# Linear-attention block with a SwiGLU feed-forward: a denser kv sum, whole-tile attention in four PSUM banks, layer-norm small ops on POOL

## Chip, cores and metric

One core of a Trainium2 chip. The metric is device time in microseconds of the whole kernel; 248.45 us is the median of three runs of the kernel before (248.22 to 249.34).

## The reference

One sequence of 2048 tokens, width 512, 32 heads of 16, feed-forward width 1376, all in bf16. `c` gives six modulation vectors.

```python
mod = (silu(c) @ w_mod)                       # -> sa, ca, ga, sb, cb, gb
h = layernorm(x) * (1 + ca) + sa
q, k, v = split(h @ wqkv)                     # 32 heads of 16
pq, pk = q @ w_phi, k @ w_phi                 # per head 16 x 16
phi = concat(softmax(p), softmax(-p))         # per head 32 features
kv, z = sum_s(phi_k * v), sum_s(phi_k)        # per head 32 x 16, 32
o = (phi_q @ kv) / (phi_q . z + 1e-6)
x = x + ga * (o @ wo)
h = layernorm(x) * (1 + cb) + sb
x = x + gb * ((silu(h @ w_gate) * (h @ w_up)) @ w_down)
```

## The kernel before

Tokens go in 16 tiles of 128 (a tile's tokens lie across the partitions), in four chunks of 512. The work falls into a first pass over all tiles, which ends in the kv sum, and a second one with attention, projection and feed-forward.

**First pass.** `first_norm` takes the mean and variance of each tile on VectorE (`stats`: two instructions), adds epsilon on VectorE, takes the power -0.5 on POOL and computes -mean*rstd on VectorE (`rstd_of`), for groups of two, two, four, four and four tiles; `normalize` runs on VectorE or ScalarE. TensorE transposes the tile, and the evacuation applies the modulation (`modulate_T`). `k_tile` multiplies by the key weights (with w_phi folded in by `fold_phi`) and the value weights; ScalarE takes exp of both signs into `e`; VectorE sums per head (`S`) and takes reciprocals (`R`); POOL multiplies (`phik`, L551). `kv_tile` adds phik^T [v, 1] into PSUM over all tiles: eight matmuls a tile, each with the 128 features of eight heads of one sign against 128 value columns and a column of ones. Three banks hold the sums: the pair `two_ps` and one single bank. `q_front` makes exp(+-q) per chunk and column block. `gate` broadcasts ga and gb, and POOL scales wo (four pieces, L626) and w_down (eleven, L630) by them as soon as they are there.

**KVZ** (`fz`, L642 and L645): VectorE multiplies the sums by a block mask and writes the matrix that the attention multiplies by: per sign and block of eight heads 128 columns of kv, eight columns of head masks and eight of z plus epsilon.

**Second pass.** `attend(n, half)` works on half a tile in the pair of banks: four matmuls, two small copies (`Ssw`), then U, den, rden, A on small operands and two multiplies `o` (L707) that read PSUM, all on VectorE (the copies on ScalarE from the third tile on). The pair is free for the next half when `o` is done. `turn` transposes the result, `project` multiplies by wo, adds to x and does the second layer norm; `second_T` transposes and modulates. `ffn_gu` does gate and up (two single banks), ScalarE silu and then either VectorE's multiply or a ScalarE copy and POOL's multiply; `ffn_down` sums eleven matmuls, and VectorE adds x. `UNITS` lists the feed-forward's units as (chunk, first tile, tiles).

**Order.** All work is given to a planner (`Plan`) as operations with engine, an estimated duration, buffers read and written. It computes due times backwards over successors (`STRETCH`, `WAIT`), the TensorE spine (`SPINE`) and the paced preparations (`PACE`, us between pairs of tiles), then places operations one by one on the engines in a simulated time and emits the instructions in that order; each engine then runs its own queue in order. `slots` says how many buffers a kind has, and `quota` how many single PSUM banks a purpose may hold. PSUM has eight banks: the pair and six single ones.

## Time and profile before

| | |
|---|---|
| profiled execution | 248.46 us |
| its span, first to last instruction | 246.7 us |
| TensorE, VectorE, ScalarE, POOL busy | 215.0, 174.6, 128.3, 101.1 us |
| mean granted TensorE clock | 0.979 |

The span was cut into four stages at 9.3 us (the modulation weights have landed), 58.4 and 72.1 us (the last kv matmul) and 92.2 us (the first gate/up matmul). A line of the stage view reads: start:end, length, busy us and instructions of TensorE's matmuls, its weight loads, VectorE, ScalarE and POOL, then the granted clock (1.00 is 2.4 GHz, with 1.2 GHz as the other level), the share of the DMA engines and GB/s. PE is TensorE, DVE VectorE, ACT ScalarE; L548 is line 548 of the kernel. A group's row gives the shapes, the count, busy time, the mean duration of one in ns, and the idle time before them with what ended it.

### The profile page before, as it was taken

Reading aid. Unit: us, or ns where it says so; the run is one execution under the profiler, and the core shown is the slowest. Engines: PE = TensorE matmul, PEld = TensorE weight load, DVE = VectorE, ACT = ScalarE, POOL = GpSimd, SP = SyncE. Lnnn points to the kernel's source line nnn. Section 1 sums busy time; section 2 is a strip of 40 time slices with the busy share of each in tenths; the row PEclk is TensorE's granted clock in tenths of the full one; section 3 lists DMA queues with packets and bytes.
Section 4 is the critical chain, followed back from the end, with each engine's and each line's share of the span. In section 5 each row is a group of like instructions: output and inputs, shape, how many; then the busy total and the mean of one; then the engine's idle time right before and its main releaser. Section 6 shows DMA issues by size and latency. Waiting matters only on the chain.

```text
span 246.7 us, 4221 instructions
## 1 busy us (share of the span) xinstructions
PE 215.0 (87%) x1533; PEld 131.7 (53%) x1556; DVE 174.6 (71%) x461; ACT 128.3 (52%) x280; POOL 101.1 (41%) x100
## 2 busy tenths in 40 slices
...
DMA packets 9062, 13.95 MB, mean 57 GB/s; under 512 B 1009, under 2 KB 6482, under 8 KB 9042
## 3 DMA queue, kind: packets, MB, share of 16 engines
...
q8 instruction: 12, 0.20, 0.3%
...
## 4 chain that ended last, share of the span: by engine, by line
PE 64%; DVE 24%; ACT 3%; DMA 3%; issue 3%; POOL 1%; SPq 0%; DVEq 0%; ACTq 0%
PE one_ps L786 31%; PE one_ps L818 14%; DVE S L548 5%; PE one_ps L748 5%; PE two_ps L675 3%; DVE st L343 3%; DMA wmod_sb<-in_w_mod_dram 3%; DVE xn L372 3%; PE one_ps L528 2%; PE one_ps L575 2%; DVE R L549 2%; PE one_ps L532 2%; DVE o L707 2%; ACT hT L396 2%; DVE ln_nmr L361 1%
## 5 line engine op out<-in xcount | busy, mean ns | idle before, releaser
L786 PE MATMUL one_ps<-hT,wg_sb 128*128 128x256 bf16 (+3 forms) x264 | 46.2, 308 | 1.2 <-ACT hT L396 0.9
L786 PE MATMUL one_ps<-hT,wu_sb 128*128 128x256 bf16 (+3 forms) x260 | 45.2, 307 | 0.2
L793 ACT ACTIVATE sg<-one_ps 128x512 bf16<-128x512 f32 (+2 forms) x46 | 26.3, 577 | 28.3 <-PE one_ps L786 25.2
L802 POOL TENSOR_TENSOR gu<-usb,sg 128x512 bf16<-128x512 bf16 (+1 forms) x22 | 23.5, 1070 | 42.7 <-ACT usb L800 39.9
L818 PE MATMUL one_ps<-wd_sb,gu 128*128 128x512 bf16 (+1 forms) x171 | 40.5, 379 | 0.2
L551 POOL TENSOR_TENSOR phik<-e,R 128x1024 bf16<-128x1024 bf16 x16 | 30.7, 1931 | 13.0 <-ACT hT L396 5.5
L786 PEld LDWEIGHTS <-wg_sb 128*128 128x128 bf16 (+1 forms) x264 | 25.9, 100 | 13.9 <-issue 2.1
L786 PEld LDWEIGHTS <-wu_sb 128*128 128x128 bf16 (+1 forms) x264 | 26.0, 100 | 12.2
L736 POOL TENSOR_TENSOR o<-o 128x512 bf16<-128x512 bf16 x14 | 16.1, 1152 | 38.0 <-DVE o L707 33.6
L796 DVE TENSOR_TENSOR gu<-one_ps,sg 128x512 bf16<-128x512 f32 (+1 forms) x24 | 16.3, 685 | 20.3 <-PE one_ps L786 18.4
L357 POOL TENSOR_TENSOR ln_rstd<-ln_veps,mhalf 128x1 f32<-128x1 f32 (+2 forms) x21 | 13.4, 639 | 38.3 <-DVE ln_veps L353 33.7
L818 PEld LDWEIGHTS <-gu 128*128 128x128 bf16 (+1 forms) x176 | 16.7, 98 | 17.0
L707 DVE TENSOR_TENSOR o<-two_ps,A 128x256 bf16<-128x256 f32 x64 | 24.0, 416 | 0.8
L343 DVE BATCH_NORM_STATS2 st<-x_c 128x6 f32<-128x512 bf16 x32 | 21.7, 679 | 2.7 <-DMA x_c<-in_A_x_dram 2.4
L581 ACT ACTIVATE eT<-one_ps 128x512 bf16<-128x512 f32 x32 | 17.5, 599 | 10.3 <-PE one_ps L575 10.3
L675 PE MATMUL two_ps<-KVZ,eT 128*128 128x144 bf16 x128 | 13.7, 232 | 7.3 <-DVE o L707 6.9
L548 DVE TENSOR_REDUCE S<-e 128x64 f32<-128x1024 bf16 x16 | 19.1, 1191 | 1.3 <-ACT e L539 1.2
L388 PE MATMUL one_ps<-ident_b,xn 128*128 128x128 bf16 x128 | 11.9, 236 | 7.1 <-DVE va L544 3.9
L528 PE MATMUL one_ps<-Wk,hT 128*128 128x512 bf16 x61 | 17.2, 399 | 1.0 <-ACT hT L396 0.6
L532 PE MATMUL one_ps<-wqkv_sb,hT 128*128 128x512 bf16 x62 | 17.1, 391 | 0.3 <-DVE st L343 0.2
L675 PEld LDWEIGHTS <-eT 128*128 128x128 bf16 x128 | 10.0, 100 | 13.6 <-DVE o L707 6.0
L748 PE MATMUL one_ps<-wo_sb,oT 128*128 128x512 bf16 x58 | 15.6, 380 | 1.7 <-ACT oT L739 1.4
...
## 6 DMA issues: line engine op xcount, KB each, us to landing
...
```

Source lines behind the costliest of these rows:

```text
L343: nc.vector.bn_stats(st6[:], src)
L528: nc.tensor.matmul(pk()[:], lhsT=hT[c_i][k][:, cols], rhs=Wk2[:, k, :], start=(k == 0), stop=(k == KD - 1))
L532: nc.tensor.matmul(v()[:], lhsT=hT[c_i][k][:, cols], rhs=wqkv_sb[:, k, 2 * D:3 * D], start=(k == 0), stop=(k == KD - 1))
L548: pl.op("DVE", r=[e], w=[Ss], us=1.18, fn=lambda: nc.vector.tensor_reduce(Ss()[:], e()[:], axis=AX.X, op=ALU.add))
L551: pl.op("POOL", r=[e, R], w=[bphik[i]], us=1.9, fn=lambda: nc.gpsimd.tensor_tensor(bphik[i]()[:], e()[:], R()[:].unsqueeze(3).to_broadcast ...
L675: nc.tensor.matmul(nd()[:, jj, sg * NDW:(sg + 1) * NDW], lhsT=eTs[c_i, sg, j][:, ts_], rhs=KVZ[:, sg * KD + j, :], start=True, stop=True)
L707: nc.vector.tensor_tensor(o2()[:, sg, half * HK:(half + 1) * HK, :].rearrange("p j (h d) -> p j h d", d=DH), ndv()[:, :, sg, 0:P].rearrang ...
L748: nc.tensor.matmul(a()[:], lhsT=oT()[:, j, :], rhs=wo_sb[:, j, :], start=(j == 0), stop=(j == KD - 1))
L786: nc.tensor.matmul(ps_()[0:fsz, q * n:(q + 1) * n], lhsT=wt[:, k, m * P:m * P + fsz], rhs=h2[k], start=(k == 0), stop=(k == KD - 1))
L793: pl.op("ACT", r=[g, bsilu], w=[sg], us=0.2 + 0.3 * L / CW, fn=lambda: nc.scalar.activation(sg()[0:fsz, 0:L], g()[0:fsz, 0:L], ACT.Silu))
L802: pl.op("POOL", r=[usb, sg], w=[gu], us=0.1 + 1.05 * L / CW, fn=lambda: nc.gpsimd.tensor_tensor(gu()[0:fsz, 0:L], usb()[0:fsz, 0:L], sg()[ ...
L818: nc.tensor.matmul(fp()[:], lhsT=b()[0:fsz, c0:c0 + P], rhs=wd_sb[0:fsz, m, :], start=(m == 0), stop=(m == FM - 1))
```

## The change

- The kv sum takes the features of four heads, both signs, in one matmul against the 64 value columns of these heads and a column of ones; eight matmuls a tile as before, with 65 columns instead of 129. The sums fit in two banks (`kv_ps`). `e`, `phik` and `va` are laid out for it, and KVZ is written in four steps, which move rows between partition halves.
- `attend(n)` does a whole tile in four banks (`four_ps`), with the same number of VectorE instructions per tile as per half before. These banks exist only after the kv sum: they take the place of `kv_ps` and of two of the six single banks, which the kinds named in `EARLY` use before.
- The first layer norm's aggregation, power and -mean*rstd run as ten small POOL instructions per group; the second one keeps the aggregation on VectorE and does the rest in four POOL instructions.
- The scaling of wo waits for the last phik, that of w_down for the first step of KVZ.
- Quotas, planner constants and estimates are others, an operation with a choice of engine takes the one that ends it first, gate operations are due before those of two groups later (`soft`), and the two two-tile units of chunk 1 become one of four.

```diff
-UNITS = [(0, 0, 2), (0, 2, 2), (1, 0, 2), (1, 2, 2), (2, 0, 4), (3, 0, 4)]
+HG = 4 * DH
+UNITS = [(0, 0, 2), (0, 2, 2), (1, 0, 4), (2, 0, 4), (3, 0, 4)]
...
-STRETCH = 1.6
-WAIT = 0.8
-SPINE = 1.2
-PACE = 11.0
+STRETCH = 2.54
+WAIT = 1.43
+SPINE = 1.1
+PACE = 8.1
+QUOTA = {'q': 2, 'turn': 4, 'T': 2, 'T2': 4, 'wo': 4, 'down': 4, 'gu': 3, 'kv': 4, 'fold': 2}
+EARLY = ("kv", "q", "fold", "T")
...
+            if b.tag == "one" and not (b.kind == f"last{i - 4}" if str(b.kind)[:4] == "last" else i < 4 or b.kind in EARLY):
+                continue
...
-    slots = {"one": 6, "two": 1, "xn": 8, "nmr": 4, "ln2": 6, "WT": 2, "e": 3, "S": 3, "R": 3, "phik": 4,
+    slots = {"one": 6, "four": 1, "xn": 8, "nmr": 4, "ln2": 6, "WT": 2, "e": 3, "S": 3, "SS": 3, "Q": 3, "R": 3, "phik": 4,
...
-    quota = {"q": 1, "turn": 1, "T": 2, "wo": 1, "down": 2, "gu": 4, "kv": 4, "fold": 3}
+    quota = QUOTA
...
-    two_ps = ps.tile([P, 2, CW], FP32, name="two_ps")
-    one_ps = [ps.tile([P, CW], FP32, name=f"one_ps{i}") for i in range(slots["one"])]
+    early_cm = tc.tile_pool(name="early", bufs=1, space=PSUM)
+    early = early_cm.__enter__()
+    kv_ps = early.tile([P, 2, CW], FP32, name="kv_ps")
+    one_ps = [ps.tile([P, CW], FP32, name=f"one_ps{i}")[:] for i in range(4)]
+    one_ps += [early.tile([P, CW], FP32, name=f"one_ps{i}")[:] for i in range(4, 6)]
+    blast = [Buf("one", kind=f"last{i}", keep=True) for i in range(2)]
+    four_ps = {}
...
-        b0, b, bn = Buf(), Buf(), Buf()
+        bn = Buf()
         st = {}
 
-        def f1():
-            st["veps"] = lnp.tile([P, n], FP32, name=name + "_veps", bufs=bufs)
-            nc.vector.tensor_scalar_add(st["veps"][:], mv_t()[:, :, 1], LN_EPS)
-
-        def f2():
+        def f():
             st["rstd"] = lnp.tile([P, n], FP32, name=name + "_rstd", bufs=bufs)
-            nc.gpsimd.tensor_tensor(st["rstd"][:], st["veps"][:], mhalf[:, 0:n], op=ALU.pow)
-
-        def f3():
             st["nmr"] = lnp.tile([P, n], FP32, name=name + "_nmr", bufs=bufs)
-            nc.vector.scalar_tensor_tensor(st["nmr"][:], in0=mv_t()[:, :, 0], scalar=-1.0, in1=st["rstd"][:],
-                                           op0=ALU.mult, op1=ALU.mult)
-        pl.op("DVE", r=bmv, w=[b0], us=0.1, fn=f1)
-        pl.op("POOL", r=[b0], w=[b], us=0.4 + 0.15 * n, fn=f2)
-        pl.op("DVE", r=[b] + list(bmv), w=[bn], us=0.1, fn=f3)
+            veps = lnp.tile([P, n], FP32, name=name + "_veps", bufs=bufs)
+            nc.gpsimd.tensor_scalar_add(veps[:], mv_t()[:, :, 1], LN_EPS)
+            nc.gpsimd.tensor_tensor(st["rstd"][:], veps[:], mhalf[:, 0:n], op=ALU.pow)
+            nc.gpsimd.tensor_scalar(veps[:], mv_t()[:, :, 0], -1.0, None, op0=ALU.mult)
+            nc.gpsimd.tensor_tensor(st["nmr"][:], veps[:], st["rstd"][:], op=ALU.mult)
+        pl.op("POOL", r=bmv, w=[bn], us=0.8 + 0.15 * n, fn=f)
...
-        pl.op([("DVE", 0.6, fd), ("ACT", 0.71, fa)], r=list(reads) + [bn], w=[bxn])
+        pl.op([("DVE", dve_us, fd), ("ACT", 0.72, fa)], r=list(reads) + [bn], w=[bxn])
...
+        st6 = lnp.tile([P, w, 6], FP32, name=f"ln1_st{n0}")
+        bst = [Buf() for _ in range(w)]
         for q in range(w):
             c_i, t = divmod(n0 + q, TPC)
-            stats(lambda q=q: mv_t()[:, q, :], x_ch[c_i][:, t, :], [bx[n0 + q]], [bmv[q]])
-        bn, rstd_t, nmr_t = rstd_of(mv_t, w, bmv, f"ln1_{n0}", 1)
+            pl.op("DVE", r=[bx[n0 + q]], w=[bst[q]], us=0.69, fn=lambda q=q, c_i=c_i, t=t: nc.vector.bn_stats(
+                st6[:, q, :], x_ch[c_i][:, t, :]))
+        tmp = lnp.tile([P, 5, w], FP32, name=f"ln1_tmp{n0}")
+        rstd = lnp.tile([P, w], FP32, name=f"ln1_rstd{n0}")
+        nmr = lnp.tile([P, w], FP32, name=f"ln1_nmr{n0}")
+        bn = Buf()
+
+        def f():
+            v = [tmp[:, i, :] for i in range(5)]
+            tt = nc.gpsimd.tensor_tensor
+            tt(v[0], st6[:, :, 1], st6[:, :, 4], op=ALU.subtract)
+            tt(v[1], st6[:, :, 2], st6[:, :, 5], op=ALU.add)
+            tt(v[2], v[0], v[0], op=ALU.mult)
+            nc.gpsimd.tensor_scalar(v[2], v[2], D / 4.0, D * LN_EPS, op0=ALU.mult, op1=ALU.add)
+            tt(v[3], v[2], v[1], op=ALU.add)
+            nc.gpsimd.tensor_scalar(v[3], v[3], 1.0 / D, None, op0=ALU.mult)
+            tt(rstd[:], v[3], mhalf[:, 0:w], op=ALU.pow)
+            tt(v[4], st6[:, :, 1], st6[:, :, 4], op=ALU.add)
+            tt(v[4], v[4], mhalf[:, 0:w], op=ALU.mult)
+            tt(nmr[:], v[4], rstd[:], op=ALU.mult)
+        pl.op("POOL", r=bst, w=[bn], us=1.6 + 0.15 * w, fn=f)
...
+            for sg in range(2):
+                nc.scalar.activation(e()[:, :, sg].rearrange("p g h f -> p g (h f)"),
+                                     pk()[:].rearrange("p (g n) -> p g n", g=G), ACT.Exp, scale=(1.0, -1.0)[sg])
...
-                sg, j = divmod(g, KD)
-                nc.tensor.matmul(kv_acc(g // 3)[:, (g % 3) * (P + 1):(g % 3 + 1) * (P + 1)],
-                                 lhsT=bphik[i]()[:, sg, 8 * j:8 * j + 8, :].rearrange("p h f -> p (h f)"),
-                                 rhs=bva[i]()[:, j, :], start=(i == 0 and g % 3 == 0), stop=(i == NT - 1),
+                nc.tensor.matmul(kv_acc(g // 4)[:, (g % 4) * (HG + 1):(g % 4 + 1) * (HG + 1)],
+                                 lhsT=bphik[i]()[:, g].rearrange("p s h f -> p (s h f)"),
+                                 rhs=bva[i]()[:, g, :], start=(i == 0 and g % 4 == 0), stop=(i == NT - 1),
                                  skip_group_check=True)
-        pl.op("PE", r=[bphik[i], bva[i]], w=bkv, us=0.46, fn=f, spine=True)
+        pl.op("PE", r=[bphik[i], bva[i]], w=[bkv], us=0.34, fn=f, spine=True)
...
+    for k in range(KD):
+        pl.op("POOL", r=[bgab[0], bphik[NT - 1]], w=[bwo[k]], us=1.16, fn=lambda k=k: nc.gpsimd.tensor_tensor(
+            wo_sb[:, k, :], wo_sb[:, k, :], gab[:, 0, :], op=ALU.mult))
...
+    bKVZ = [Buf() for _ in range(4)]
+    for sg in range(2):
+        for r in range(2):
+            def fz(sg=sg, r=r):
+                src = kv_ps[HG * sg:HG * sg + HG, 0:2, 0:4 * (HG + 1)].rearrange("p b (g n) -> p b g n", g=4)[:, :, r::2, :]
+                dst = KVZ[HG * r:HG * r + HG, KD * sg:KD * sg + KD, :].rearrange("p (b g) n -> p b g n", b=2)
+                rows = slice(HG * sg, HG * sg + HG)
+                nc.vector.tensor_tensor(dst[:, :, :, HG * r:HG * r + HG], src[:, :, :, 0:HG],
+                                        bm4[rows, :].unsqueeze(1).unsqueeze(1).to_broadcast([HG, 2, 2, HG]), op=ALU.mult)
+                for b in range(2):
+                    nc.vector.scalar_tensor_tensor(dst[:, b, :, P + 8:P + 16],
+                                                   in0=src[:, b, :, HG:HG + 1].to_broadcast([HG, 2, 8]),
+                                                   scalar=0.5 * DEN_EPS,
+                                                   in1=bmz[rows, r, :].unsqueeze(1).to_broadcast([HG, 2, 8]),
+                                                   op0=ALU.add, op1=ALU.mult)
+            pl.op("DVE", r=[bkv], w=[bKVZ[2 * sg + r]], us=0.65, fn=fz)
+
+    for m in range(FM):
+        fsz = fm_size(m)
+        pl.op("POOL", r=[bgab[1]] + bKVZ[0:1], w=[bwd[m]], us=1.16, fn=lambda m=m, fsz=fsz: nc.gpsimd.tensor_tensor(
+            wd_sb[0:fsz, m, :], wd_sb[0:fsz, m, :], gab[0:fsz, 1, :], op=ALU.mult))
...
+        early_cm.__exit__(None, None, None)
+        four_ps[0] = ctx.enter_context(tc.tile_pool(name="late", bufs=1, space=PSUM)).tile([P, KD, CW], FP32, name="four_ps")
...
+    pl.op("NONE", r=bKVZ + bgab + [bmodB, bmodA] + bWq2, w=[bturn] + blast, us=0.0, fn=f_turn)
...
-        nd = pair()
-        js = [half * HK + jj for jj in range(HK)]
+        nd = Buf("four", lambda slot: four_ps[0])
 
         def fn():
-            for jj, j in enumerate(js):
+            for j in range(KD):
                 for sg in range(2):
-                    nc.tensor.matmul(nd()[:, jj, sg * NDW:(sg + 1) * NDW], lhsT=eTs[c_i, sg, j][:, ts_],
+                    nc.tensor.matmul(nd()[:, j, sg * NDW:(sg + 1) * NDW], lhsT=eTs[c_i, sg, j][:, ts_],
                                      rhs=KVZ[:, sg * KD + j, :], start=True, stop=True)
-        pl.op("PE", r=[beT[c_i, sg, j] for j in js for sg in range(2)] + bKVZ + [bturn], w=[nd], us=0.25, fn=fn)
+        pl.op("PE", r=[beT[c_i, sg, j] for j in range(KD) for sg in range(2)] + bKVZ + [bturn], w=[nd],
+              us=0.5, fn=fn)
...
+        pl.op([("ACT", 0.18, lambda: fs(nc.scalar.copy)), ("DVE", 0.22, lambda: fs(nc.vector.tensor_copy))],
+              r=[nd], w=[Ssw])
+        pl.op("DVE", r=[nd, Ssw], w=[A], us=1.15, fn=fa)
+        o2 = bo2[n] = sb("qf", "o2", [P, 2, KD, P], BF16)
...
-                nc.vector.tensor_tensor(o2()[:, sg, half * HK:(half + 1) * HK, :].rearrange("p j (h d) -> p j h d", d=DH),
+                nc.vector.tensor_tensor(o2()[:, sg].rearrange("p j (h d) -> p j h d", d=DH),
                                         ndv()[:, :, sg, 0:P].rearrange("p j (h d) -> p j h d", d=DH),
-                                        A()[:, :, sg, :].unsqueeze(3).to_broadcast([P, HK, 8, DH]), op=ALU.mult)
-        if half == 0:
-            pl.op("DVE", r=[nd, A], w=[o2], us=0.7, fn=fo)
-        else:
-            pl.op("DVE", r=[nd, A], w=[second], us=0.7, fn=fo)
-            o2.users.append(pl.ops[-1])
+                                        A()[:, :, sg, :].unsqueeze(3).to_broadcast([P, KD, 8, DH]), op=ALU.mult)
+        pl.op("DVE", r=[nd, A], w=[o2], us=1.25, fn=fo)
...
+        for o in pl.ops[gu_ops[-2]:gu_ops[-1]] if len(gu_ops) > 1 else ():
+            o.soft.append(first)
...
+        for n in (2 * k, 2 * k + 1):
+            attend(n)
+        for n in (2 * k, 2 * k + 1):
+            turn(n, k == 0)
+            project(n)
```

## Rows read from the trace of the kernel before

**Rows 1.** Busy time by stage, A to D: us, each engine's busy us (instructions), granted clock.

```profile
9.30:58.37 49.07, 41.67 (x360) 26.45 (x366) 46.67 (x84) 37.21 (x69) 34.05 (x24) 0.94 0.50 184
58.37:72.10 13.73, 13.06 (x91) 7.11 (x92) 8.69 (x12) 8.79 (x17) 12.21 (x8) 0.95 0.00 1
72.10:92.20 20.10, 14.65 (x92) 7.61 (x92) 16.27 (x61) 10.62 (x24) 6.01 (x7) 0.92 0.00 1
92.20:243.40 151.20, 143.51 (x974) 88.72 (x987) 98.26 (x290) 68.46 (x167) 46.89 (x50) 1.00 0.04 14
```

**Rows 2.** The chain of waits in order of time: start, us, what.

```profile
17.05 1.23 DVE S L548
...
57.12 1.09 DVE S L548
...
73.29 0.42 PE two_ps L675 x4
...
215.69 10.74 PE one_ps L786 x49
```

**Rows 3.** Groups by line, VectorE, 9.3 to 72.1 us: busy us, mean ns | idle before.

```profile
L548 DVE TENSOR_REDUCE S<-e 128x64 f32<-128x1024 bf16 x16 | 19.1, 1191 | 1.3 <-ACT e L539 1.2
...
L549 DVE RECIPROCAL R<-S 128x64 f32<-128x64 f32 x16 | 8.8, 547 | 0.9
L372 DVE TENSOR_SCALAR xn<-x_c,ln_mv,ln_rstd 128x512 bf16<-128x512 bf16 x9 | 7.7, 896 | 0.0
...
L361 DVE SCALAR_TENSOR_TENSOR ln_nmr<-ln_mv,ln_rstd 128x4 f32<-128x4 f32 (+1 forms) x4 | 3.5, 882 | 0.0
L344 DVE BATCH_NORM_AGGREGATE ln_mv<-st 128x2 f32<-128x6 f32 x14 | 2.5, 182 | 0.5
...
L353 DVE TENSOR_SCALAR ln_veps<-ln_mv 128x4 f32<-128x4 f32 (+1 forms) x4 | 1.9, 464 | 0.1
```

**Rows 4.** VectorE in order of time, two normalizations: start, us, line, what.

```profile
50.34 3.56 DVE L372 TENSOR_SCALAR xn<-x_c,ln_mv,ln_rstd 128x512 bf16<-128x512 bf16 x2
...
90.46 0.41 DVE L372 TENSOR_SCALAR xn<-x_c,ln,ln_rstd 128x512 bf16<-128x512 bf16 x1
```

**Rows 5.** Groups by line, POOL, 9.3 to 72.1 us.

```profile
L551 POOL TENSOR_TENSOR phik<-e,R 128x1024 bf16<-128x1024 bf16 x16 | 30.7, 1931 | 13.0 <-ACT hT L396 5.5 <-DVE R L549 3.9 <-PE one_ps L558 2.4
L630 POOL TENSOR_TENSOR wd_sb<-wd_sb,gab 128x512 bf16<-128x512 bf16 x7 | 8.1, 1171 | 0.0
...
L357 POOL TENSOR_TENSOR ln_rstd<-ln_veps,mhalf 128x4 f32<-128x4 f32 (+1 forms) x4 | 3.7, 931 | 5.6 <-DVE ln_veps L353 5.5
```

**Rows 6.** Groups by line and shape, POOL, whole span.

```profile
L323 POOL MEMSET va<- 128x4 bf16 x4 | 0.2, 117 | 0.0
```

**Rows 7.** The chain of waits, two runs of small matmuls.

```profile
9.32 1.02 PE one_ps L434 x32
...
61.56 0.35 PE two_ps L558 x6
```

**Rows 8.** VectorE in order of time, KVZ and the first attention steps.

```profile
72.04 0.56 DVE L642 TENSOR_TENSOR KVZ<-two_ps,bm 128x384 bf16<-128x384 f32 x1 [2.72 <-PE two_ps L558]
...
75.13 0.81 DVE L695 TENSOR_TENSOR A<-Ssw,rden 128x32 f32<-128x32 f32 x1
...
77.75 0.19 DVE L690 TENSOR_TENSOR U<-two_ps,Ssw 128x32 f32<-128x32 f32 x1
...
78.69 0.75 DVE L707 TENSOR_TENSOR o<-two_ps,A 128x256 bf16<-128x256 f32 x2
80.17 0.17 DVE L685 COPY Ssw<-two_ps 128x16 f32<-128x16 f32 x1 [0.73 <-PE two_ps L675]
```

**Rows 9.** Groups by line, whole span.

```profile
L796 DVE TENSOR_TENSOR gu<-one_ps,sg 128x512 bf16<-128x512 f32 (+1 forms) x24 | 16.3, 685 | 20.3 <-PE one_ps L786 18.4 <-PE one_ps L735 1.9
...
L793 ACT ACTIVATE sg<-one_ps 128x512 bf16<-128x512 f32 (+2 forms) x46 | 26.3, 577 | 28.3 <-PE one_ps L786 25.2 <-issue 1.2 <-DVE o L707 1.1
```

**Rows 10.** Waits of TensorE in stage D: total us, times, longest.

```profile
PE two_ps L675 <- DVE o L707: 2.8, 2, 1.7
```

137 lines of the change are left out of this document (53 added, 84 removed).

## The prediction

> **What bounds the kernel now.** I read the span by stage first, then the chain of waits, then the groups of instructions stage by stage, and last the order in time of VectorE around the stalls. Four stages stand out [rows 1]. In A (9.3 to 58.4 us, layer norm, keys, values and most of the kv sum) VectorE is busy 46.67 of 49.07 us while TensorE's record shows gaps and a granted clock of 0.94; in B (58.4 to 72.1, the last four key tiles and six kv steps) TensorE is busy 13.06 of 13.73. In C (72.1 to 92.2, from the last kv matmul to the first gate/up matmul) no engine is full: TensorE 14.65 of 20.1, VectorE 16.27. In D (92.2 to 243.4, the feed-forward with the remaining attention beside it) TensorE is busy 143.51 of 151.2. The chain of waits says the same: it runs over VectorE's reduction from 17.05 to 57.12 us, reaches the attention through KVZ at 73.29, and ends in long runs of gate/up matmuls such as 49 in 10.74 us [rows 2]. So A is VectorE's, C is a chain of hand-offs, D is TensorE's with 7.7 us of gaps. Before 9.3 us a weight load from DRAM decides, and nothing in the change touches it; the last 3.3 us are one add and one store.
>
> **First stage, layer norm.** What VectorE does between 9.3 and 72.1 us [rows 3]: 16 reductions (19.1 us) and reciprocals (8.8), nine normalizations (7.7), and the small layer-norm work that the change takes off it: ln_nmr 3.5, ln_veps 1.9, aggregates 2.5. The aggregates overlap their neighbours a little, so I count 2.0 for them: 3.5 + 1.9 + 2.0 = 7.4 us removed. The small ops are dear (882 and 464 ns mean) because some of them stand until a POOL instruction is over; so do normalizations: two took 3.56 us at 50.34 [rows 4], against 0.41 us for one at 90.46 that meets no POOL work. If all nine cost 0.4, 7.7 would be 3.6, so 0 to 4.1 us more could go. I take 1.0 of it: POOL's load in A and B is 34.05 + 12.21 = 46.3 us [rows 1], of which phik is 30.7 and the powers 3.7 [rows 5]; the other 11.9 are the eleven wo and wd scalings that the change moves behind the kv sum, but ten small ops per group come in. VectorE's sum is then 55.4 - 7.4 - 1.0 = 47.0 us. It was busy for 88% of the 62.8 us; at that share 47.0 need 53.4, 9.4 us less.
>
> That isn't all to be had, because the next engines stand close: ScalarE has 46.0 us in the same stretch [rows 1], TensorE 54.7 with some q matmuls and stretched records in it, and POOL 46.3 - 11.9 = 34.4 plus the new small ops. No row shows such an op on POOL apart from the power; bounds are a fill of 117 ns [rows 6] and the power over up to four columns, 931 ns [rows 5]. Nine new ops in three groups (the fourth and fifth, two tiles each, lie early) are 27 x 0.12 = 3 us to 27 x 0.93 = 25 us; nearest in kind is the fill, since a power is an iterated function, and I take 0.2 us each, 5 us, which leaves POOL at about 40. With three engines between 40 and 47 us, hand-offs rather than VectorE alone set the pace, so I take 6.5 of the 9.4 us; ends for the range: 2 (POOL or ScalarE becomes the bound) and 9.4.
>
> **kv sum.** A tile takes eight matmuls of 129 columns, six of them 0.35 us on the chain, 58 ns each; the new ones have 65 columns. No such row exists. The 32 one-column matmuls with a weight load each took 1.02 us, 32 ns each [rows 7], so a tile's kv step costs between 8 x 32 = 0.26 and 8 x 58 = 0.46 us. 64 columns less at 2.4 GHz are 27 ns, which gives 31 ns, so I take 0.26 us. It counts only where TensorE is full: six steps in B, 6 x 0.2 = 1.2 us at most, and B loses part of its pressure; I take 0.8 (0 to 1.2). The page "TensorE: Matmul & The Clock Gate" of the Trainium skill, section "Back-to-back issue gap", lets a sequencer cost of about 62 ns per matmul bind below 64 columns when hardware decode is off; by that the kv step would not get shorter and the total would be 0.8 us worse. The 32 ns row says that it doesn't bind here.
>
> **KVZ.** Before, the first two of three mask-and-copy pairs start at 72.04 and the first attention matmul at 73.29 [rows 2, 8]. The new one has four steps, each a multiply of 256 elements out of PSUM (an o multiply of that size takes 0.75 / 2 = 0.38 us [rows 8]) and two small ops of 0.1 to 0.19: 4 x 0.65 = 2.6, and then the matmuls. All of it is on the path, as nothing of the attention can start. Cost: +1.0 us (0.6 to 1.4).
>
> **Attention step, stage C.** Before, a half tile costs VectorE 0.94 us for U, den, rden and A (77.75 to 78.69) and 0.75 us for o, and the next half's first copy starts only at 80.17 because there is one pair of banks: 2.7 us a half, 5.4 a tile [rows 8]. Whole: the four small ops have twice the columns, a few hundredths each and about 0.1 for the reciprocal (16 columns now; 64 take 0.55 [rows 3]), so 1.15; o is two multiplies of 512 elements, 0.685 us in the like row for gu [rows 9], 1.3; two copies 0.2; then 1.2 for release, eight matmuls and hand-over: 3.85 us a tile. Two tiles stand ahead of the first gate/up matmul: 2 x 1.55 = 3.1 us less. Against it: the 15 scalings of 1.17 us [rows 5] now all run behind the kv sum, where five ran before. While one runs, A takes 0.81 us, where in the next half all four small ops took 0.94 [rows 8], and den, too, reads its operands from SBUF and is held; before, only the first half met this, now both tiles do: +1.0. The layer-norm ops of the second tile wait behind a scaling on POOL's queue: +0.6. Together -1.5 (ends -3.1 and +1.5). The q matmuls are filler here in both kernels, and ScalarE's exponentials with them.
>
> **Feed-forward, stage D.** VectorE loses 2 x 1.69 - 2.45 = 0.9 us per tile in the attention and 0.35 in small ops: 14 tiles, 17 us of its 98.3 [rows 1]. TensorE's 7.7 us of gaps are what that can give back; attention matmuls waiting for o are 2.8 of them [rows 10]. One unit boundary fewer (two two-tile units become one of four) and a closer pace of preparation (8.1 us instead of 11) work on the rest. But single banks fall from six to four, gate/up may hold three instead of four, and all else shares what is left. I take -2.5, the near end being -5; the far end is the slower rival below.
>
> **Sum.** The profiled execution took 248.46 us, span 246.7 and 1.76 around it; the median is 248.45, so no correction. 248.46 - 6.5 - 0.8 + 1.0 - 1.5 - 2.5 = 238.2 us, own range 233 to 242.5.
>
> **Rivals.**
> *A second engine takes over stage A.* POOL's small ops cost nearer to 0.5 us than 0.2 (27 x 0.5 = 13.5, POOL at 48 us and each group's normalization late by 5 us), or ScalarE with more normalizations fills up. For it: VectorE, ScalarE and POOL end within 7 us of each other in my sum. Against: POOL's folds of 11.9 us leave the stage. Then 2 us instead of 6.5: 242.7. The Trainium skill's "GPSIMD Engine Reference", section "Engine selection", sends element-wise work to VectorE, since POOL is about half as fast on two inputs; by an estimate from that factor 7.4 us moved become 15 on POOL, which points to this rival. The rows bear it out only for the power.
> *Everything comes through.* VectorE's 9.4 us in full, D's gaps -5, C -3.1 with no stalls: 248.46 - 9.4 - 0.8 + 1.0 - 3.1 - 5 = 231.2. For it: the gaps in D are hand-offs behind VectorE. Against: three engines nearly level in A.
> *Bank shortage in D, slower.* With three gate/up banks a group of 0.87 us can start when the bank of three groups back is free. An up-projection bank is released by VectorE (0.685 us [rows 9]) or ScalarE after silu (0.58 [rows 9]); with hand-over this comes about 0.95 us after its last matmul, and the next use of the bank 1.74 us after it: 0.8 us of slack, where four banks gave 1.65. VectorE's o pair is now 1.3 us, and if the multiply stands behind it the slack is gone by 0.5 us. There are 45 gate/up pairs (two units of 6, three of 11). D would then lose its 2.5 us and more; at 0.17 us a pair (7.8 / 45) the change is worth nothing, at 0.27 the time is 248.46 - 7.8 + 12.2 = 252.9. For it: few banks while projection, transposes and down share the fourth. Against: TensorE now waits for no gate/up bank in any listed wait, and VectorE has 17 us more room.
>
> **How the numbers follow.** The forecast has 0.52, the second engine 0.20, everything through 0.14, the bank shortage 0.08, and 0.06 lies near no change by partial losses. No change means within 0.5% (1.24 us, what a measurement here can tell). Faster 0.52 + 0.20 + 0.14 = 0.86, same 0.06, slower 0.08. The range leaves out the fastest 0.06 and the slow 0.13: 231 to 247.5.
>
> **What would show it.** In the changed trace the last kv matmul should end near 65 us, not 72; VectorE's busy share up to there should stay above 85%; phik should be followed closely on POOL by the scalings, with den and A of the first two tiles at 0.5 to 0.8 us. Small POOL ops at 0.1 to 0.3 us bear out the first stage, at 0.5 or more the second engine. The kv group should read near 32 ns a matmul. First gate/up about 19 us after the last kv matmul. In D, gate/up runs should stay at 0.219 us a matmul (10.74 / 49 now); gaps between groups released by gu, usb or sg mean the bank shortage, and a stage D longer than 151 us makes the prediction wrong, as does a last kv matmul after 70 us.

## The result and the profile after

The changed kernel takes 230.2 us (median of four runs, 229.9 to 230.4) against 248.3 us in the same session: a ratio of 0.928, 95% interval [0.922, 0.933]. The forecast was 238.2, so the sign was right and 8 of the 18 us gained were not foreseen; the time lies 0.8 us below the low end of the range. In e4 below three of four executions, in e12 one of four, were over 1.5% longer than the fastest of the same kernel; so e4 has no ratio, the ratio of e12 is that of the other three, and the profile of e12, which is of the longest, gives no amounts. The profiled execution has a span of 228.6 us at a mean granted clock of 1.000, where before it was 246.7 at 0.979.

The windows view of the changed kernel, with the same four stages (columns as in [rows 1]: A from the first modulation matmul, B the last 13 us of the kv sum, C from there to the first gate/up matmul, then D):

```profile
8.80:49.40 40.60, 34.69 (x316) 20.63 (x317) 36.09 (x53) 34.99 (x63) 28.49 (x51) 1.00 0.62 227
49.40:62.50 13.10, 12.74 (x137) 6.77 (x135) 9.76 (x14) 11.12 (x23) 12.92 (x8) 1.00 0.00 1
62.50:83.50 21.00, 17.78 (x121) 9.30 (x119) 16.83 (x42) 17.20 (x35) 19.21 (x24) 1.00 0.00 1
83.50:225.24 141.74, 139.92 (x883) 78.51 (x880) 84.90 (x186) 63.55 (x128) 55.70 (x91) 1.00 0.05 15
```

Beside [rows 1]: A and B together went from 62.8 to 53.7 us (-9.1), C from 20.1 to 21.0 (+0.9), D from 151.2 to 141.7 (-9.5), and the start is 0.5 shorter. In A VectorE, which was busy 46.67 of 49.07 us, is now at 36.09 of 40.60. In B it is GpSimd (12.92 of 13.10). In D TensorE's gaps fell from 7.7 to 1.8 us (141.74 - 139.92), and its busy time from 143.5 to 139.9.

The chain of waits of the changed kernel (start, us, what), to be held against [rows 2] and [rows 7]:

```profile
26.63 3.82 POOL phik L584 x2
30.44 0.16 POOL ln_tmp L519
...
31.88 1.04 POOL ln_rstd L525
...
33.69 2.31 DVE xn L388 x2
...
54.80 0.26 PE kv_ps L591 x8
...
60.12 1.94 POOL phik L584
62.10 0.43 PE kv_ps L591 x8
62.53 2.60 PE one_ps L608 x12
65.14 0.67 PE four_ps L710 x8
...
83.67 2.62 PE one_ps L816 x24
...
124.48 12.09 PE one_ps L816 x56
```

In the first pass the chain runs through GpSimd's phik and the ten small layer-norm operations that now follow one another on its queue, no longer from one VectorE reduction to the next. A kv step of eight matmuls takes 0.26 us where TensorE is full, 33 ns a matmul; where it has waited for phik the step shows 0.43. Gate/up runs at 12.09 / 56 = 0.216 us a matmul (0.219 before).

The groups of VectorE that answer to [rows 3], 8.8 to 62.5 us (busy us, mean ns | idle before):

```profile
L580 DVE TENSOR_REDUCE S<-e 128x64 f32<-128x1024 bf16 x16 | 19.2, 1198 | 0.8 <-ACT e L570 0.4
L582 DVE RECIPROCAL R<-S 128x64 f32<-128x64 f32 x16 | 8.3, 536 | 0.8
...
L388 DVE TENSOR_SCALAR xn<-x_c,ln_rstd,ln_nmr 128x512 bf16<-128x512 bf16 x7 | 7.4, 1087 | 1.6 <-POOL ln_nmr L528 1.6
```

And of GpSimd in the same stretch, for [rows 5]: phik as before, the power, and one of the nine small operations.

```profile
L584 POOL TENSOR_TENSOR phik<-e,R 128x1024 bf16<-128x1024 bf16 x16 | 30.5, 1932 | 4.3 <-ACT e L570 2.2 <-ACT va L576 1.9 <-DVE R L582 0.2
L525 POOL TENSOR_TENSOR ln_rstd<-ln_tmp,mhalf 128x4 f32<-128x4 f32 (+1 forms) x4 | 3.8, 956 | 0.3
...
L524 POOL TENSOR_SCALAR ln_tmp<-ln_tmp 128x4 f32<-128x4 f32 (+1 forms) x4 | 0.9, 228 | 0.3
```

The ln_nmr, ln_veps and aggregate groups have left VectorE; the small operations cost GpSimd 0.20 to 0.23 us each. The normalizations that stayed on VectorE are no cheaper (1087 ns mean, 896 before).

What TensorE waits for in the first pass, and then in D (total us, times, longest):

```profile
PE kv_ps L591 <- POOL phik L584: 5.3, 5, 2.1
```
```profile
PE one_ps L404 <- DVE xn L388: 1.1, 2, 0.6
PE one_ps L404 <- ACT xn L392: 0.7, 2, 0.3
```

The wait for phik is new in this size (1.0 us before), so GpSimd's phik is what the kv sum now waits for last; e7 shows that this is not a bound by GpSimd's load. In D the listed waits before were 2.8 us for o [rows 10], 1.8 for xn, 0.9 for oT and 0.9 for hT. After, only those for xn are left, 1.8 us in all, and no wait for a gate/up bank is listed.

VectorE in order of time around KVZ and in the first and a later attention tile, for [rows 8]:

```profile
62.57 0.42 DVE L671 TENSOR_TENSOR KVZ<-kv_ps,bm 64x256 bf16<-64x256 f32 x1 [2.50 <-PE kv_ps L591]
...
64.72 0.26 DVE L674 SCALAR_TENSOR_TENSOR KVZ<-kv_ps,bmz 64x16 bf16<-64x16 f32 x2
...
66.46 1.23 DVE L728 TENSOR_TENSOR den<-U 128x32 f32<-128x32 f32 x1
...
68.12 0.73 DVE L731 TENSOR_TENSOR A<-Ssw,rden 128x64 f32<-128x64 f32 x1
68.88 1.29 DVE L739 TENSOR_TENSOR o<-four_ps,A 128x512 bf16<-128x512 f32 x2
...
84.29 0.19 DVE L728 TENSOR_TENSOR den<-U 128x32 f32<-128x32 f32 x1
...
84.91 0.23 DVE L731 TENSOR_TENSOR A<-Ssw,rden 128x64 f32<-128x64 f32 x1
```

While GpSimd scales weights, den takes 1.23 and A 0.73 us in the first tile (0.64 and 0.73 in the second); after it has finished, 0.19 and 0.23.

Last, stage D in windows of 10 us. Columns as in [rows 1]; first three windows of the kernel before, then two of the changed kernel in which VectorE is busy with attention steps:

```profile
152.00:162.00 10.00, 8.31 (x79) 7.24 (x81) 8.87 (x32) 5.43 (x16) 4.07 (x5) 1.00 0.01 2
...
192.00:202.00 10.00, 9.94 (x55) 4.96 (x54) 8.79 (x27) 3.71 (x12) 4.47 (x5) 1.00 0.00 0
...
212.00:222.00 10.00, 8.10 (x42) 3.82 (x43) 3.36 (x8) 4.28 (x8) 1.71 (x2) 1.00 0.04 13
```
```profile
142.00:152.00 10.00, 10.00 (x66) 5.48 (x65) 8.78 (x18) 4.13 (x9) 4.52 (x7) 1.00 0.00 1
...
182.00:192.00 10.00, 10.00 (x55) 4.80 (x54) 9.23 (x19) 2.46 (x5) 4.84 (x12) 1.00 0.04 13
```

After the change TensorE stays full in the windows in which VectorE is busiest. Before, with VectorE busy 8.9 of 10 us, TensorE had 8.3 in one window, but 9.9 in another with VectorE at 8.8; and 4 of its 7.7 us of gaps stand in two windows, from 172 and from 212 us on (the second is shown), in which VectorE is busy 6.1 and 3.4 us. There a unit ends, and TensorE waits for xn and hT, in the first also for o. So VectorE's load in a window does not tell by itself whether TensorE gets a gap. Another difference to see is the number of VectorE instructions: 32 and 27 in ten microseconds before, 18 and 19 after.

### The profile page after: what moved, and what is told of

It reads as the page before. It is cut to its first block, busy times and chain, and to the rows that moved or that the text cites. A ratio compares the mean times of both kernels' runs of the same rounds, so it can differ in the third digit from the quotient of the medians.

```text
span 228.6 us, 3976 instructions
## 1 busy us (share of the span) xinstructions
PE 207.3 (91%) x1468; PEld 117.0 (51%) x1468; DVE 153.8 (67%) x311; ACT 129.9 (57%) x251; POOL 121.1 (53%) x194
## 4 chain that ended last, share of the span: by engine, by line
PE 65%; DVE 13%; POOL 12%; issue 4%; DMA 3%; ACT 1%; SPq 0%; DVEq 0%; POOLq 0%; ACTq 0%
PE one_ps L816 33%; PE one_ps L851 10%; PE one_ps L776 6%; POOL phik L584 5%; PE four_ps L710 4%; PE one_ps L608 3%; DMA wmod_sb<-in_w_mod_dram 3%; DVE S L580 3%; PE one_ps L563 2%; DVE xn L388 2%; POOL ln_rstd L378 2%; PE one_ps L404 2%; PE one_ps L763 1%; PE one_ps L559 1%; DVE R L582 1%
## 5 line engine op out<-in xcount | busy, mean ns | idle before, releaser
L816 PE MATMUL one_ps<-hT,wg_sb 128*128 128x512 bf16 (+3 forms) x220 | 45.7, 336 | 0.0
L816 PE MATMUL one_ps<-hT,wu_sb 128*128 128x512 bf16 (+3 forms) x220 | 45.4, 336 | 0.0
L829 DVE TENSOR_TENSOR gu<-one_ps,sg 128x512 bf16<-128x512 f32 (+1 forms) x24 | 16.5, 689 | 36.6 <-PE one_ps L816 36.2
L816 PEld LDWEIGHTS <-wu_sb 128*128 128x128 bf16 (+1 forms) x220 | 21.8, 100 | 16.1
L816 PEld LDWEIGHTS <-wg_sb 128*128 128x128 bf16 (+1 forms) x220 | 21.4, 100 | 15.0 <-issue 0.3
L739 DVE TENSOR_TENSOR o<-four_ps,A 128x512 bf16<-128x512 f32 x32 | 20.6, 686 | 0.6
L392 ACT ACTIVATE xn<-x_c,ln_nmr,ln_rstd 128x512 bf16<-128x512 bf16 x18 | 14.2, 809 | 11.5 <-POOL ln_nmr L380 8.3
L570 ACT ACTIVATE e<-one_ps 128x512 bf16<-128x512 f32 x32 | 17.1, 603 | 1.4 <-PE one_ps L559 1.1
L857 DVE TENSOR_TENSOR ot<-x_c,one_ps 128x512 bf16<-128x512 bf16 x16 | 10.9, 680 | 7.1 <-PE one_ps L851 7.0
L608 PE MATMUL one_ps<-hT,Wq 128*128 128x512 bf16 x64 | 15.4, 379 | 0.0
L833 ACT CAST usb<-one_ps 128x512 bf16<-128x512 f32 (+1 forms) x21 | 11.9, 565 | 5.3 <-PE one_ps L816 5.3
```

Source lines behind the costliest of these rows:

```text
L570: nc.scalar.activation(e()[:, :, sg].rearrange("p g h f -> p g (h f)"), pk()[:].rearrange("p (g n) -> p g n", g=G), ACT.Exp, scale=(1.0, - ...
L608: nc.tensor.matmul(pq()[:], lhsT=Wq2[:, k, j * P:(j + 1) * P], rhs=hT[c_i][k][:], start=(k == 0), stop=(k == KD - 1))
L739: nc.vector.tensor_tensor(o2()[:, sg].rearrange("p j (h d) -> p j h d", d=DH), ndv()[:, :, sg, 0:P].rearrange("p j (h d) -> p j h d", d=DH ...
L816: nc.tensor.matmul(ps_()[0:fsz, q * n:(q + 1) * n], lhsT=wt[:, k, m * P:m * P + fsz], rhs=h2[k], start=(k == 0), stop=(k == KD - 1))
```

## The experiments

The stages of every run, from the profile: from the first modulation matmul to the last kv matmul (A+B), to the first gate/up matmul (C), to the last matmul (D). All in us; the ratio is to the kernel before in the same session, whose median was 247.3 to 248.5.

```
kernel                      time    ratio [95%]            A+B    C     D
before                      248.3                          62.8  20.1  151.1
changed                     230.2   0.928 [0.922, 0.933]   53.7  21.0  141.7
e1  old constants           234.5   0.947 [0.942, 0.952]   54.1  22.8  143.9
e2  half tiles              247.4   0.999 [0.996, 1.002]   53.8  24.3  155.1
e3  LN small ops on VectorE 239.2   0.966 [0.962, 0.970]   55.0  21.3  147.1
e4  scalings early          240.7   -                      55.7  20.1  143.8
e5  half tiles, old const.  247.0   0.994 [0.988, 1.000]   54.7  25.7  153.5
e6  planner part alone      256.5   1.033 [1.028, 1.038]   57.1  20.9  164.8
e7  aggregate on VectorE    233.7   0.942 [0.937, 0.948]   53.2  21.5  144.0
e8  w_down scaling later    233.3   0.939 [0.934, 0.944]   53.0  20.7  144.1
e9  half, gate/up off DVE   253.9   1.027 [1.021, 1.032]   53.8  24.3  161.9
e10 dummy VectorE work      240.1   0.971 [0.965, 0.978]   54.0  22.5  151.0
e11 no scalings             230.8   0.931 [0.924, 0.938]   54.1  18.5  145.4
e12 one query bank          243.2   0.982 [0.974, 0.989]   53.1  23.6  154.9
e13 half, shorter chain     237.3   0.956 [0.948, 0.965]   53.1  22.4  148.0
e14 e13 padded              241.6   0.975 [0.967, 0.982]   52.9  22.7  151.4
e15 before, two query banks 247.8   0.998 [0.994, 1.002]   63.3  21.2  149.4
```

One caution for all of them: the order of every engine's work comes out of the planner, so an edit in one place reorders the rest. D moved by 2.3 to 5.4 us in e3, e7 and e11, whose edits all lie ahead of it. A difference of that size in D is not yet the work of an edit.

**e1, the planner's constants of before in the changed kernel.**

```diff
-STRETCH = 2.54
-WAIT = 1.43
-SPINE = 1.1
-PACE = 8.1
+STRETCH = 1.6
+WAIT = 0.8
+SPINE = 1.2
+PACE = 11.0
```

> The changed kernel with the four planner constants of before (STRETCH 1.6, WAIT 0.8, SPINE 1.2, PACE 11), all else as changed. Theory P (the feed-forward stage lost its gaps because preparation is placed earlier by the planner): 234 to 238 us, stage D 145 to 150 us instead of 141.7, with gaps at the unit boundaries. Rival V (VectorE's relief and the whole-tile step closed the gaps): within 1.5 us of 230.2, D under 143.5.

Measured: 234.5 us, so the constants are worth 4.3 us here, 1.8 of it in C and 2.2 in D. The time is in the first theory's range, D (143.9) in neither's. In D they are at most a small part of the 9.5.

**e2, half tiles.** The attention step of before in the changed kernel: two tiles of two banks in place of one of four; all else stays.

```diff
-        nd = Buf("four", lambda slot: four_ps[0])
+        nd = Buf("four", lambda slot: four_ps[0][:, HK * slot:HK * slot + HK, :])
...
-            attend(n)
+            attend(n, 0)
+            attend(n, 1)
```

> The changed kernel with attention by half tiles, the four banks used as two pairs (VectorE instructions per tile doubled, two buffers). Theory V: VectorE's 0.95 us a tile comes back and hits stage D: 234 us or more, D over 145. Theory P: the double buffer covers it, 229 to 232.5, D under 143.5; stage C may get shorter because the second half's matmuls no longer wait for o.

Measured: 247.4 us. All 17 us are gone again, although the first pass keeps its 9 us: D grows to 155.1 and C to 24.3. Stage D of this kernel as a whole and one window of it (windows view), and its first wait of TensorE from 84 us on:

```profile
87.39:242.45 155.06, 144.94 (x889) 78.81 (x887) 97.09 (x277) 65.98 (x145) 56.08 (x91) 0.99 0.04 14
112.00:122.00 10.00, 8.54 (x80) 6.71 (x79) 9.04 (x30) 4.20 (x13) 4.29 (x4) 1.00 0.00 1
```
```profile
PE four_ps L712 <- DVE o L742: 4.3, 6, 1.2
```

VectorE is back at 97.1 us with 277 instructions (84.9 with 186), and TensorE has 10.1 us of gaps.

**e5, half tiles with the old constants**, the two edits above together.

> Half-tile attention in two pairs of banks, and the four old planner constants, all else as changed; with the two runs that undid one of the two it completes a square. Theory V (the whole-tile step itself is worth 10 us or more, since half tiles make TensorE wait in its queue for o, whatever the constants): 245 to 252 us. Rival P2 (the new constants are only bad for half tiles): 236 to 241, so that a half tile costs 2 to 6 us under constants that suit it.

Measured: 247.0 us. With half tiles the constants make no difference (247.4 and 247.0), with whole tiles 4.3 us; the whole tile is worth 12.5 us with the old constants and 17.2 with the new ones.

**e6, the kernel before with the planner's part of the change alone**: constants, choice of engine by the earliest end, soft due times, units.

```diff
-                    cand.setdefault(eng, []).append((t, o.due, o.n, o, alt, rooms))
+                    got.append((t + alt[1], t, alt))
+                _, t, alt = min(got, key=lambda x: x[0])
+                cand.setdefault(alt[0], []).append((t, o.due, o.n, o, alt, rooms))
```

> The kernel before with only the planner part of the change: constants, choice of engine by earliest end, soft edges, and one four-tile unit for chunk 1. Theory V: no gain, 246 to 251 us, since the attention by half tiles still blocks TensorE's queue. Rival P (the planner closes the gaps): 238 to 244, stage D under 147.

Measured: 256.5 us, 8 slower than before. D is 13.7 us longer, but A and B are 5.7 shorter (62.8 to 57.1): another order alone gives the first pass more than half of its 9.1 us, with the old kv sum and VectorE's small operations in place. In all the planner's part gains only together with the new attention step.

**e3, the first layer norm's small operations back on VectorE**, and the second's stay on GpSimd.

```diff
+        pl.op("DVE", r=bmv, w=[b0], us=0.1, fn=f1)
+        pl.op("POOL", r=[b0], w=[b], us=0.4 + 0.15 * n, fn=f2)
+        pl.op("DVE", r=[b] + list(bmv), w=[bn], us=0.1, fn=f3)
...
-        pl.op("POOL", r=bst, w=[bn], us=1.6 + 0.15 * w, fn=f)
```

> The changed kernel with the first layer norm's aggregation, epsilon and -mean*rstd on VectorE again (power on POOL). Theory L (VectorE's small ops made the first stage shorter): the last kv matmul ends at 67 to 70 us instead of 62.5, total 235 to 238. Rival S (the wo and w_down scalings behind the kv sum freed POOL, and so VectorE's stalls): it ends at 61 to 64.5, total 229 to 232.5, as POOL loses 1.9 us of small ops a group.

Measured: 239.2 us. The last kv matmul ends at 66.1 instead of 62.5 us, and 2.3 of these 3.6 lie ahead of A: in TensorE's order of time the first transposes, which wait for xn, now stand in front of the modulation matmuls (start, us, line, what [idle before]):

```profile
9.70 0.29 PE L425 MATMUL one_ps<-ident_b,xn 128*128 128x128 bf16 x1 [1.95 <-ACT xn L413]
...
11.12 1.03 PE L471 MATMUL one_ps<-silucT,wmod_sb 128*128 128x1 bf16 x32
```

So moving the small operations is worth 3.6 us of the first pass at most, 1.3 of them within A and B. They are no longer dear on VectorE in this order (groups of VectorE, to be held against ln_nmr in [rows 3], 882 ns each):

```profile
L398 DVE SCALAR_TENSOR_TENSOR ln_nmr<-ln_mv,ln_rstd 128x4 f32<-128x4 f32 (+1 forms) x4 | 0.5, 114 | 0.8 <-POOL ln_rstd L394 0.8
```

VectorE's load in A and B is 46.3 us here and 45.9 in the changed kernel. D's 5.4 us more come with the other order of the plan and a granted clock of 0.77 from 85 to 100 us; they say nothing about the layer norm.

**e7, the first layer norm's aggregation on VectorE with the four GpSimd operations of the second layer norm**, instead of ten GpSimd operations.

```diff
-            pl.op("DVE", r=[bx[n0 + q]], w=[bst[q]], us=0.69, fn=lambda q=q, c_i=c_i, t=t: nc.vector.bn_stats(
-                st6[:, q, :], x_ch[c_i][:, t, :]))
...
+            stats(lambda q=q: mv_t()[:, q, :], x_ch[c_i][:, t, :], [bx[n0 + q]], [bmv[q]])
+        bn, rstd_t, nmr_t = rstd_of(mv_t, w, bmv, f"ln1_{n0}", 1)
```

> The changed kernel with the first layer norm's mean and variance aggregated on VectorE (16 more instructions of 0.1 to 0.18 us) and four POOL instructions a group instead of ten. If POOL bounds the first stage now (chain through phik and the ten small ops), 1.7 us a group go: last kv matmul at 59 to 61.5 instead of 62.5, total 227 to 229.5. If VectorE still bounds it, 62.5 to 64.5, total 230 to 232.

Measured: A+B 53.2, the start 1.0 later, the last kv matmul at 63.1 us, the kernel 233.7, which is above both ranges. GpSimd is busy 36.8 us in A and B instead of 41.4, and they are 0.5 us shorter: its load does not bound the first pass. Where the aggregation is done is nearly level on both engines.

**e4 and e8, the scalings of the weights earlier and later.** In e4 those of w_o and w_down are ready to go beside the kv tiles; in e8 those of w_down wait for the first tile's second layer norm.

```diff
-        pl.op("POOL", r=[bgab[1]] + bKVZ[0:1], w=[bwd[m]], ...)
+        pl.op("POOL", r=[bgab[1]], w=[bwd[m]], ...)              # e4 (w_o the same)
+        pl.op("POOL", r=[bgab[1]] + [bxn2[0]], w=[bwd[m]], ...)  # e8
```

> The changed kernel with the wo and w_down scalings ready for POOL from the seventh tile on, as before. Theory S: eleven or more scalings of 1.17 us go into the first stage, where POOL is busy nearly all the time now: last kv matmul at 70 us or later, total 235 or more. Theory L: VectorE is the bound there, so under 65 us, total 229 to 232, and stage C loses its stalls of den and A (about 2 us).

Measured: one execution took 233.6 us and three 240.1 to 241.9, so its verdict stays open. The profile is of the first: the last kv matmul ends at 64.6 us, A+B is 2.0 us longer, C 0.9 shorter.

> The changed kernel with the w_down scalings placed on POOL only after the first tile's second layer norm is normalized, so that the first attention tiles meet only the four wo scalings. If the scalings' hold on den and A (1.0 and 0.5 us a tile) sits on the path of stage C: C 18.5 to 20 us instead of 21.0, total 228 to 229.5. If TensorE's q matmuls fill C anyway: no change within 1 us, or slower if the scalings now delay the second layer norm of the second tile or the first down matmul.

Measured: 233.3 us; C 0.3 and A+B 0.7 shorter, D 2.4 longer, as the second branch had it. VectorE in order of time in the first tile:

```profile
66.04 0.19 DVE L724 TENSOR_TENSOR den<-U 128x32 f32<-128x32 f32 x1
...
66.65 0.22 DVE L727 TENSOR_TENSOR A<-Ssw,rden 128x64 f32<-128x64 f32 x1
```

Nothing holds den and A here, and still C is only 0.3 us shorter.

**e11, no scalings at all** (both loops taken out; the output lacks the gates).

> The changed kernel without the scalings of the output and down weights by their gates on GpSimd (15 multiplies, 16 us; left out, so the output lacks the gates). Theory of the hold (GpSimd's multiplies hold VectorE's small operations: den 1.23 and A 0.73 to 1.18 us beside them, 0.19 and 0.23 without): the stage from the last kv matmul to the first gate/up (21.0 us) falls by 1 to 3 us, its den and A fall to about 0.2 to 0.3 us each, the kernel to 227 to 229.5. Rival (that stage is set by TensorE, 17.8 of 21.0 us busy with 14 query groups in it, and by the wait for the second layer-norms): it stays within 0.7 us, kernel 229.5 to 231.

Stage C (windows), and two small operations of its first tile (VectorE in order of time):

```profile
62.86:81.33 18.47, 17.68 (x122) 9.34 (x120) 13.48 (x42) 16.81 (x35) 2.87 (x9) 1.00 0.00 1
```
```profile
66.80 0.19 DVE L721 TENSOR_TENSOR den<-U 128x32 f32<-128x32 f32 x1
...
67.41 0.22 DVE L724 TENSOR_TENSOR A<-Ssw,rden 128x64 f32<-128x64 f32 x1
```

The hold of single operations is shown: den is 0.19 where it was 1.23, and C is 2.5 us shorter, as the first theory had it. What the hold costs C is not: e8 lifts it as well and has 0.3 us, and here GpSimd's queue is also free for the second layer norm. The time is 230.8 us, because D became 3.7 longer. Why D takes it back I can't show.

**e9, half tiles with all gate/up multiplies off VectorE.**

```diff
-        if (ms[0] * w // TPC) % 2 == 0:
+        if False:
```

> The half-tile kernel (247.4 us, last stage 155.1) with one more edit: none of the gate/up multiplies runs on VectorE; all go through a ScalarE copy and a GpSimd multiply. It takes 24 x 0.69 = 16.5 us from VectorE's 97.1 in the last stage and leaves the half tiles, their bank pairs and TensorE's work as they are. Theory (VectorE bursts: in the 10 us before a chunk's gate/up run VectorE is busy 8.5 to 9.3 of 10 and TensorE waits for it): the last stage falls by 6 to 10 us, to 145 to 149, and the kernel to 237 to 241. Rival (a half tile blocks TensorE's queue by its bank pair, whatever else VectorE has to do): last stage within 2 us of 155, kernel 245 or more. A result between says that both hold a part.

Stage D and its first wait from 84 us on:

```profile
86.77:248.66 161.89, 144.60 (x889) 79.11 (x887) 89.51 (x259) 76.53 (x163) 83.28 (x115) 0.99 0.04 13
```
```profile
PE four_ps L712 <- DVE o L742: 10.5, 7, 1.6
```

A miss for the theory, and a D longer than its rival allowed for: 253.9 us. VectorE lost only 7.6 us (97.1 to 89.5) of the 16.5. A, and den with it, became longer beside GpSimd's 24 further multiplies (groups of VectorE in D, e2 and then e9):

```profile
L732 DVE TENSOR_TENSOR A<-Ssw,rden 128x32 f32<-128x32 f32 x26 | 6.7, 258 | 0.9
```
```profile
L732 DVE TENSOR_TENSOR A<-Ssw,rden 128x32 f32<-128x32 f32 x26 | 10.6, 408 | 0.9
```

That is 3.9 us, den adds 1.9 (7.9 to 9.8), and four more normalizations on VectorE 2.0. Both operations stand in a half's chain, and the waits for its banks rose from 4.3 to 10.5 us. So load, hold and hand-off all changed here, and this run tells nothing about VectorE's load by itself.

**e10, the changed kernel with dummy work on VectorE.**

```diff
-        pl.op("DVE", r=[nd, A], w=[o2], us=1.25, fn=fo)
+            for i, m in enumerate((512, 192)):
+                dm = pools["qf"].tile([P, 6], FP32, name=f"dm{i}", bufs=2)
+                nc.vector.bn_stats(out=dm[:], in_=wg_sb[:, 0, 0:m])
+        pl.op("DVE", r=[nd, A], w=[o2], us=2.2, fn=fo)
```

> The changed kernel (230.2 us) with two idle reads of a constant tile added on VectorE behind the multiplies of each attention tile (512 and 192 columns, some 0.67 and 0.28 = 0.95 us a tile, 15.2 us in all, 12.4 of it in the last stage, results thrown away). That brings VectorE's load in the last stage from 84.9 back to about 97, as with half tiles, with whole tiles kept. Theory (bursts): although the mean load stays at 97 of 142, the last stage grows by 5 to 13 us and the kernel comes to 236 to 244. Rival (it was the hand-offs and banks of half tiles, not VectorE's load; the mean says there is room): last stage within 2 us, kernel 229 to 233.5, of which up to 2 us in the stage of the first attention tiles, where the 0.95 us stand in each tile's chain.

Stage D and two windows of it:

```profile
85.40:236.40 151.00, 144.68 (x882) 79.59 (x880) 92.11 (x204) 62.29 (x130) 55.29 (x91) 0.98 0.04 14
122.00:132.00 10.00, 6.17 (x45) 3.32 (x44) 9.39 (x24) 4.35 (x9) 4.74 (x13) 0.98 0.07 26
132.00:142.00 10.00, 10.00 (x41) 4.25 (x40) 3.02 (x6) 4.16 (x7) 3.45 (x3) 0.85 0.00 1
```

As the theory had it: the dummies measure 0.68 and 0.34 us, 13.4 in D (13 tiles), and D grows by 9.3 us, 4.5 of gaps and 4.8 of longer busy time, although VectorE's mean load is only 92 of 151. The second row shows a place where it happens: a burst in which VectorE has 9.4 of 10 us and TensorE 6.2, with waits for x_c, gu, hT and xn; the third that the granted clock is 0.85 behind that gap (0.50, the 1.2 GHz level, from 132 to 134 us), while VectorE has 3 us to do. A mean over a stage is no cover.

**e13 and e14, an attempt to part load and hand-off in the half tile.** e13 leaves two of the five VectorE steps of a half out (part of the denominator is missing); e14 puts as much VectorE time back behind the multiplies, where it no longer delays that half's own banks.

```diff
-            nc.vector.tensor_tensor(U[:], ndv()[:, :, :, P + 8:P + 16], Ssw()[:], op=ALU.mult)
-            nc.vector.tensor_tensor(den[:], U[:, :, 0, :], U[:, :, 1, :], op=ALU.add)
-            nc.vector.reciprocal(rden[:], den[:])
+            nc.vector.reciprocal(rden[:], Ssw()[:, :, 0, :])
...
+            nc.vector.bn_stats(out=dm[:], in_=wg_sb[:, 0, 0:320])     # e14 only, after o
```

> The half-tile kernel (247.4 us, last stage 155.1) without two of the five VectorE steps of each half: the product with the other sign's sums (0.19 us) and their addition (0.30 us); the reciprocal is taken of one sum directly (part of the denominator is left out). It takes 4.8 + 7.9 = 12.7 us of VectorE's 97.1 from the last stage and 0.49 us from the chain between a half's attention matmuls and the release of its banks. Load theory (VectorE's work comes in bursts that are VectorE-bound; the dummies of the whole-tile kernel cost 9.3 us of last stage for 14.4 us, 0.65 each): last stage 146 to 148, kernel 238 to 241. Hand-off theory (TensorE stands at a half's matmuls until the half two before it is multiplied): the last stage falls as well, by 4 to 9 us. If neither VectorE's load nor the chain matters: within 2 us of 247.

> The kernel with the shortened chain of a half, with an idle read of 320 columns of a constant tile (about 0.48 us) behind the multiplies of each half on VectorE, so that VectorE's load is that of the half-tile kernel again (28 x 0.48 = 13.4 us back) while banks are still released 0.49 us earlier after the matmuls (the same part of the denominator is left out). Load theory: last stage back to 153 to 157, kernel 245.5 to 249.5, 6 us or more above the shortened one. Hand-off theory: within 2.5 us of the shortened one.

Stage D of e13 (windows) and its first wait of TensorE from 84 us on, then the same of e14:

```profile
84.28:232.32 148.04, 142.60 (x889) 78.82 (x887) 86.06 (x229) 63.44 (x135) 55.82 (x91) 1.00 0.04 14
```
```profile
PE four_ps L712 <- DVE o L738: 2.2, 4, 0.7
```
```profile
84.79:236.23 151.44, 142.87 (x888) 78.71 (x887) 98.37 (x260) 62.75 (x136) 55.95 (x91) 1.00 0.04 14
```
```profile
PE four_ps L712 <- DVE o L738: 4.8, 9, 1.2
```

Neither theory holds alone; 241.6 lies between their bounds. From e2 to e14 the load is nearly the same (97.1, 98.4) and the banks come free earlier: D 155.1 to 151.4, 3.7 us. From e14 to e13 12.3 us of VectorE work go: D to 148.0, 3.4 us. Each of these steps lies within what a reordering alone does to D; together, 7.1 us, they lie outside it. And e13 with VectorE at 86.1 us is still 6.3 us above the whole tile with 84.9: what is left may be that a half tile has twice as many steps, matmuls and releases that go back and forth between TensorE and VectorE (229 VectorE instructions against 186). That this rest is hand-off is argued, not shown: 3.6 of it are gaps of TensorE (5.4 against 1.8), 2.7 longer busy time.

**e12, one bank for query projections in the changed kernel.**

```diff
-QUOTA = {'q': 2, 'turn': 4, ...
+QUOTA = {'q': 1, 'turn': 4, ...
```

> The changed kernel with one bank for query projections where it has two, so that they are spread out: five of the 16 groups (5 x 0.865 = 4.3 us of TensorE) move from the first two stages into the last one. Theory (filler taken early is a gain, because the last stage is bound by TensorE and the stage before it has idle time): the last stage grows by about 4.3 us, to 146, the stage of the first attention tiles shortens by less than 2 us, the kernel comes to 232.5 to 235. Rival (where the query groups stand makes no difference to the total, what leaves one stage shortens the other): kernel 229.5 to 231.5.

Stage D, in the execution of 245.8 us:

```profile
85.70:240.59 154.89, 148.93 (x898) 82.49 (x896) 85.01 (x183) 67.46 (x132) 54.73 (x90) 0.97 0.04 14
```

The other three took 242.1 to 244.1 us, so the kernel is 12 to 13 us slower than the changed one, about three times what the theory took (4.3). Five query groups stand in D, as expected, and VectorE's load there is that of the changed kernel (85.0 and 84.9). So the early query groups are a second condition of the gain. By what way is not shown: the mean granted clock is 0.965 in this execution and 0.984 to 0.992 in the other three, which have no profile, and the quota changes the order of the whole plan.

**e15, two banks for query projections in the kernel before.**

```diff
-    quota = {"q": 1, "turn": 1, ...
+    quota = {"q": 2, "turn": 1, ...
```

> The kernel before with one number changed: two banks for query projections in place of one, by which none of the 16 groups is left for the last stage (three were there, 3 x 0.865 = 2.6 us of TensorE). Theory (the early query groups are a part of the last stage's 9.4 us of gain by themselves): last stage 148.5 or less, at most 1.5 us more in the stage of the first attention tiles, kernel 245 to 247. Rival (in the kernel before, TensorE has 9.5 us of idle time in the last stage, which hides them; the gain comes only where the half tiles' VectorE work has gone): last stage within 1 us of 151.1, kernel 247.5 to 250.

```profile
93.37:242.78 149.41, 143.14 (x976) 88.01 (x975) 98.33 (x290) 62.80 (x157) 46.63 (x50) 0.99 0.04 14
```

The kernel takes 247.8 us (ratio 0.998 [0.994, 1.002]): D gives 1.7 us and the stages ahead take it back (C +1.1, A+B +0.5). Early query groups gain nothing while half tiles stand in D.

## Why the prediction was wrong, step by step

- **First pass, -7.3 forecast, -9.1 measured: the size was near, the way was not.** The prices held: small operations cost 0.2 us on GpSimd (0.20 to 0.23 measured), a kv matmul 32 ns (33 measured). But the 6.5 us were to come from taking 7.4 us of small operations off VectorE. With them back on it (e3) A and B are only 1.3 us longer, 3.6 with the later start, as ln_nmr takes 114 ns there and not 882. And the planner's part alone makes A and B of the kernel before 5.7 us shorter (e6). So most of what ln_nmr cost, the dearest of them, was standing, and another order removes that; the near sum is in part luck. The denser kv sum was not tried by itself, so its share is open. Two query groups less in A and B (two against four), 2 x 0.865 = 1.7 us of TensorE, are a part that the sum did not have. The kv end came at 62.5 us where 65 was named. Normalizations did not get cheaper, so the -1.0 us taken for them was wrong.
- **Rules beside the rows.** The Trainium skill's "TensorE: Matmul & The Clock Gate", section "Back-to-back issue gap", names about 62 ns a matmul as the bound up to 64 columns when hardware decode is off. The chain shows 33 ns for 65 columns with a weight load each, so this bound was not met here. The estimate from the Trainium skill's "GPSIMD Engine Reference", section "Engine selection", was 15 us on GpSimd; the nine small lines sum to 7.6 us and the power to 3.8, which it took before as well (3.7).
- **KVZ, +1.0 forecast.** From the kv end to the first attention matmul it was 1.2 us and is now 2.6: +1.4, the end of the range given. The prediction's own terms, 2.6 us against 73.29 - 72.04 = 1.25, give +1.35; it took less without a reason.
- **Stage C, -1.5 without KVZ, about -0.5 measured** (0.9 - 1.4). The steps of a whole tile are as worked out (1.13 us from U to o and 1.29 for o when nothing is held). The scalings do hold den and A, but what that costs C, 1.0 + 0.6 in the sum, is open: with the hold lifted C is 0.3 us shorter in e8 and 2.5 in e11. C also took in five more query groups (14 against 9), 4.3 us of TensorE, without growing by more than 0.9 us: that they are filler there was right. That they stay "in both kernels" where they were was not looked at, and was wrong.
- **Stage D, -2.5 forecast with -5 as the near end, -9.5 measured. This is the step that failed**, and two readings in it. First, "TensorE's 7.7 us of gaps are what that can give back" is the right pool, and 5.9 of it came back (7.7 to 1.8): the waits for o, oT and hT, 4.6 us together, are gone. I valued the pool at a third because the load was spread over the stage (98 of 151 us looked like room) and the listed wait for o was 2.8 us. e2 shows that half tiles cost 13.4 us of D, so that without the whole tile nothing of D's gain is left (155.1 us against 151.1 before). e10 shows that 13.4 us of VectorE work more cost D 9.3 at a mean that has room. How much of the half tile's cost is VectorE's load and how much hand-off stays open: e13 takes 7.1 us of it back by a shorter chain and less load together, 6.3 are left. The relief itself was 13.4 us of VectorE (98.3 to 84.9) where 17 had been taken. Second, TensorE's busy time was taken as fixed; it fell by 3.6 us, of which three query groups (2.6 us) left D for C. e12 shows that this is a condition of the gain, e15 that it gains nothing by itself.
- **The rivals.** "Everything comes through" (231.2 us) was nearest, and its reason, gaps in D that are hand-offs behind VectorE, fits the waits that went and e2 and e10. Its first-pass term, VectorE's 9.4 us in full, is met by the number (9.1) and not by the way (e3, e6). "Bank shortage" is refuted: no wait for a gate/up bank is listed in D, with three of them. "A second engine takes over" is not borne out: the kv sum does wait for GpSimd's phik, but 4.6 us less on GpSimd (e7) shorten A and B by 0.5.

The parts do not add. Taken back alone, the whole tile costs 17.2 us, the second query bank 12 to 13, the constants 4.3, the layer norm's small operations up to 9.0: more than twice the 18.1 us gained. Put alone into the kernel before, the second query bank gives nothing and the planner's part loses 8 us.
